# A recurrent layer's state decay: eight ScalarE activations by head in place of one GpSimd product

## The chip, the cores and the metric

The kernel runs on one core of a Trainium2 chip. The core has five engines with instruction streams of their own: TensorE (PE, with its weight loads PEld), VectorE (DVE), ScalarE (ACT), GpSimd (POOL) and SyncE (SP, which here only issues DMAs). Each engine takes its instructions in order; between engines, semaphores hold an instruction until its inputs are there. The metric is the device time of one execution in microseconds (us), as the median of several runs.

## The reference: what is computed

Three layers follow one another: a recurrent layer with a decaying state (batch 4, 8 heads, 768 steps, head size 48), a mixture of eight experts with a skip test, and a dense layer that multiplies by a clipped gate. The change is in the first:

```python
state = np.zeros((B, H, D, D))
for t in range(S):
    kt, vt, rt = k[:, :, t], v[:, :, t], r[:, :, t]
    cur = np.einsum('bhd,bhe->bhde', u[None] * kt, vt)
    y[:, :, t] = np.einsum('bhd,bhde->bhe', rt, state + cur)
    state = w[None, :, :, None] * state + np.einsum('bhd,bhe->bhde', kt, vt)
```

The decay `w` has one value for each head and each of the 48 rows of the state.

## The kernel before, in words

The recurrence is done in 12 chunks of 64 steps (`C = 64`, `NCH = 12`). Within a chunk the steps are matrix products; from one chunk to the next only the state goes on, multiplied by `w` to the 64th power. The state lies in `SS[c % 2]`, a float32 tile with 112 partitions (48 rows of the state for one pair of batches, 16 unused, 48 rows for the other pair) and 2 x 8 x 48 = 768 elements (two batches side by side, head, column). `T` ("Tpow" in the profile) holds powers of `w` by head, and column 96 of it is the 64th.

For TensorE, VectorE, ScalarE and GpSimd the order of instructions is the order of the program text; the DMAs on SP keep theirs as well. Pass i of the loop over chunks (from line 551) puts in the queues, in this order:

- SP: the store of the rows of chunk i-1 (`store`, L472), the load of values for chunk i+2 (`load_v`, L317).
- `powers(i+2)` (L398): the queries of chunk i+2 are multiplied by powers on GpSimd, the keys on VectorE; both 112 x 1024, in place in `RK`. GpSimd can begin when the load of `RK` (L311) is there.
- `scores(i+1, 0)` on TensorE (L417) and `place(i+1, 0)` on VectorE (L422), which copies them under masks from PSUM tile `at` into `ZZ`. There is one `at`, so the next scores wait for the copies.
- `bonus(i+2)` on ScalarE (L404): eight activations, one for each head, 112 x 128 each, with a scale for each partition. They read what GpSimd made in `powers`.
- `chunk(i)`: `grow` (L431, key-value products into PSUM tiles `sp`), `state` on VectorE (L438): the new state is `sd` + `sp`; then `inner` (L451), which writes the output banks `yp`.
- `settle` on ScalarE (L458), `logits(i-2)` (matmuls L492, copies on ScalarE L494), the loads of the next `KN` and `RK` on SP.
- `scores(i+1, 1)`, `place(i+1, 1)`; `keys(i+2)` on GpSimd (L409).
- `decay(i+1)` (L444): `sd` is the new state times its decay. It is done for i+1 = 1 to 10, ten times. The next reader of `sd` is `state(i+1)`, one pass later.
- `turn(i-1)` on TensorE (L478), then `split(i-1)`: `xh` on ScalarE (L484) and `xl` on VectorE (L485).
- `outer(i)` on TensorE (L464), the state's share of the output, and `evac(i)` on ScalarE (L469), which empties `yp` into `xs`; the next `inner` has to wait for it.

In passes 7 to 10 the routing of the first tokens is worked out besides, mainly on VectorE (L79 to L195), and in passes 9 to 11 ScalarE begins to split weights of the first expert (L706, L708, in the function `unit`). When the loop ends, the experts follow (to about 313 us of the profile), and then the dense layer.

Of the kernel before, what the change touches and what calls it, by code (L numbers as in the profile page):

```python
# [15 lines left out]
AF = mybir.ActivationFunctionType  # L16
ALU = mybir.AluOpType
# [3 lines left out]
B, H, S, D = 4, 8, 768, 48  # L21
# [184 lines left out]
class Kernel:  # L206
# [70 lines left out]
    def attention(self):  # L277


        nc, tc = self.nc, self.tc  # L280
        with ExitStack() as ctx:
# [14 lines left out]
            SS = [flat(t) for t in S_]  # L296
            ZZ = [cst.tile([128, 2, H, C], F32, name=f"ZZ{i}") for i in range(2)]
            sd = cst.tile([112, 2, H, D], F32, name="sd")
# [48 lines left out]
            T = cst.tile([112, H, 128], F32, name="Tpow")  # L347
# [18 lines left out]
                                        inv[:, :, i:i + 1].to_broadcast([112, H, n]), op=ALU.mult)  # L366
                n, i = 2 * n, i + 1
            PRb = T[:, :, 0:64].unsqueeze(1).to_broadcast([112, 2, H, C])
            dec = T[:, :, 96:97].unsqueeze(1).to_broadcast([112, 2, H, D])
            uw = cst.tile([112, H], F32, name="uw")  # L370

            mask = self.mask
# [68 lines left out]

            def decay(c):

                nc.gpsimd.tensor_tensor(sd, SS[c % 2], dec, op=ALU.mult)  # L444

            def inner(c, yp):

# [103 lines left out]
            for i in range(NCH):  # L551
# [48 lines left out]
                if not last and i + 1 < NCH - 1:  # L600
                    decay(i + 1)
# [712 lines left out]
```

## Time and profile before

| what | value |
|---|---|
| time, median of 3 runs (lowest to highest) | 680.26 us (676.86 to 681.88) |
| the profiled execution: its own time | 687.5 us |
| its span, from the first to the last instruction | 685.6 us |
| instructions | 15680 |
| busy share of the span: PE, DVE, ACT, POOL | 92%, 57%, 47%, 17% |

A busy share is an average over stages with different limits. "Idle before, releaser" is the time for which an engine stood still ahead of an instruction, and what ended it. "Issue" is time in which an engine waited for nothing that the profile shows. The granted clock of TensorE is given as a share of its full 2.4 GHz; the lower of its two levels is 1.2 GHz, and a mean between 0.5 and 1 is a mix of the two.

### The profile page before, as it was taken

To read this page: it belongs to the slowest core of one execution; us is meant where nothing else is said; L and a number is where in the kernel's file an instruction comes from. 1 tells how busy PE (TensorE), PEld (TensorE's weight loads), DVE (VectorE), ACT (ScalarE), POOL (GpSimd) and SP (SyncE) were. 2 spreads that over 40 slices of the span, in tenths; PEclk is the share of its full clock that TensorE was granted. 3 is DMA by queue.
4 is the path that set the end of the run, shared out by engine and by line. 5 is a ranking of instruction groups with operands and counts; after the bars stand their busy time and mean duration, and the time that the engine had idled before them with its cause. 6 is when DMAs were issued, how large, how long until landed. Compare 5 with 4: busy or idle time off the path is not lost.

```text
span 685.6 us, 15680 instructions
## 1 busy us (share of the span) xinstructions
PE 632.0 (92%) x6728; PEld 406.2 (59%) x6728; DVE 392.6 (57%) x643; ACT 319.7 (47%) x603; POOL 119.9 (17%) x83
## 2 busy tenths in 40 slices
PE   8687777687998999999999999999999999999996
PEld 4576766675776777755555555555555555555553
DVE  7565447959488998479974343334334343434332
ACT  2354434584477656354563344335433533443332
POOL 4675644433721113100000000000000000000000
PEclk9688567889999999999999999999999999999999
DMA  8987885173868777155512010201010010002002
GB/s 249 274 225 215 211 217 159 49 230 123 313 233 297 269 258 253 52 169 206 187 45 46 1 35 12 46 1 47 7 41 1 1 44 3 1 1 47 1 0 47
DMA packets 25229, 79.13 MB, mean 115 GB/s; under 512 B 3906, under 2 KB 13252, under 8 KB 23364
## 3 DMA queue, kind: packets, MB, share of 16 engines
q1 hardware_dynamic: 22964, 70.22, 33.5%
q0 software_dynamic: 2192, 7.87, 3.3%
q8 instruction: 54, 0.88, 0.5%
q14 instruction: 19, 0.16, 0.1%
HBM read 65.49 MB, written 12.58 MB: 114 GB/s over the span
## 4 chain that ended last, share of the span: by engine, by line
PE 65%; DVE 13%; DMA 11%; issue 6%; ACT 3%; SPq 1%; POOL 0%; POOLq 0%; DVEq 0%; ACTq 0%
PE a L1110 26%; PE y L1128 13%; PE s L1128 13%; DMA raw<-in_w 5%; PE at L417 4%; DVE wl L711 4%; DMA X<-xg,icol 2%; PE g L478 2%; PE y L464 2%; PE y L451 2%; PE s L431 1%; DMA xg<-X,icol 1%; DVE ZZ L422 1%; ACT wh L706 1%; DVE hl L758 1%
## 5 line engine op out<-in xcount | busy, mean ns | idle before, releaser
L1110 PE MATMUL a<-x,wih 128*128 128x512 f16 x480 | 142.8, 379 | 0.0
L1115 DVE SCALAR_TENSOR_TENSOR g<-r,a 128x512 f32<-128x512 f32 x96 | 65.9, 686 | 133.9 <-ACT r L1113 133.9
L1113 ACT ACTIVATE r<-a,half_c 128x512 f32<-128x512 f32 x96 | 65.7, 685 | 126.1 <-PE a L1110 126.0
L1128 PEld LDWEIGHTS <-gh 128*128 128x128 f16 x768 | 75.1, 98 | 54.5
L1119 ACT ACTIVATE gh<-g 128x512 f16<-128x512 f32 x96 | 60.6, 631 | 86.8 <-DVE g L1115 86.8
L1120 DVE SCALAR_TENSOR_TENSOR gl<-g,gh 128x512 f16<-128x512 f32 x96 | 66.3, 691 | 57.9 <-ACT gh L1119 57.9
L1110 PE MATMUL a<-x,wil 128*128 128x512 f16 x240 | 91.0, 379 | 0.0
L1110 PEld LDWEIGHTS <-wih 128*128 128x128 f16 x576 | 55.5, 98 | 55.7 <-issue 0.2
L753 PE MATMUL a<-mx,wh 128*128 128x128 f16 (+1 forms) x576 | 68.0, 241 | 3.7 <-DVE hl L758 2.8
L1128 PE MATMUL y<-woh,gl 128*128 128x384 f16 x192 | 62.6, 326 | 0.3 <-DVE gl L1120 0.3
L1128 PE MATMUL y<-woh,gh 128*128 128x384 f16 x192 | 62.6, 326 | 0.0
L1128 PE MATMUL y<-wol,gh 128*128 128x384 f16 x192 | 62.6, 326 | 0.0
L1128 PE MATMUL s<-woh,gh 128*128 128x384 f16 x192 | 62.6, 326 | 0.0
L1128 PE MATMUL s<-woh,gl 128*128 128x384 f16 x192 | 62.6, 326 | 0.0
L1128 PE MATMUL s<-wol,gh 128*128 128x384 f16 x192 | 62.6, 326 | 0.0
L753 PE MATMUL a<-mx,wl 128*128 128x128 f16 (+1 forms) x288 | 60.4, 241 | 0.0
L711 DVE SCALAR_TENSOR_TENSOR wl<-raw,wh 128x768 f16<-128x768 f32 x57 | 52.8, 966 | 9.2 <-ACT wh L706 9.1
L422 DVE COPY_PREDICATED ZZ<-mask,at 128x512 f32<-128x512 uint8 x48 | 35.2, 734 | 38.6 <-PE at L417 37.7
L706 ACT ACTIVATE wh<-raw 128x768 f16<-128x768 f32 x64 | 50.9, 838 | 11.8 <-DMA raw<-in_w 11.6
L1128 PEld LDWEIGHTS <-gl 128*128 128x128 f16 x384 | 37.6, 98 | 30.4 <-DVE gl L1120 0.9
L753 PEld LDWEIGHTS <-wh 128*128 128x128 f16 x576 | 49.6, 99 | 9.9 <-issue 3.4
L417 PE MATMUL at<-RK 48*64 48x128 f32 x768 | 39.4, 353 | 12.7 <-DVE ZZ L422 8.2
(199 smaller groups left out, 969.4 us busy)
## 6 DMA issues: line engine op xcount, KB each, us to landing
raw<-in_w SPq DMA_DIRECT2D x13, 1536.0 KB, 6.8
RK<-in_rkT SPq DMA_DIRECT2D x32, 192.0 KB, 5.9
draw<-in_win SPq DMA_DIRECT2D x8, 768.0 KB, 5.0
draw<-in_wout SPq DMA_DIRECT2D x8, 768.0 KB, 4.3
KN<-in_kn SPq DMA_DIRECT2D x12, 384.0 KB, 6.1
VV<-in_vn SPq DMA_DIRECT2D x12, 384.0 KB, 4.8
X<-xs SPq DMA_DIRECT2D x12, 384.0 KB, 4.2
out<-o SPq DMA_DIRECT2D x48, 96.0 KB, 2.2
```

The lines of the kernel that those rows point to most:

```text
L417: nc.tensor.matmul(at[tok(b), TG[b], j], x[dim(b), 1, DG[b], h], x[dim(b), 0:3:2, DG[b], h], start=True, stop=True)
L422: nc.vector.copy_predicated(ZZ[c % 2][:, :, 4 * hh:4 * hh + 4], mask[:, m].unsqueeze(1).unsqueeze(1).to_broadcast([128, 2, 4, C]), at[:, : ...
L451: nc.tensor.matmul(yp[b // 2][out(b), h], z[tok(b), TG[b], h], v[tok(b), cols(TG[b], h)], start=h == 0, stop=c == 0 and h == H - 1, skip_g ...
L706: nc.scalar.activation(hi, src, AF.Copy, scale=SW)
L711: nc.vector.scalar_tensor_tensor(lo, src, SW, hi, op0=ALU.mult, op1=ALU.subtract)
L753: nc.tensor.matmul(hp[:, j], a[:, kc, fs], b[:, kc], start=(k == 0), stop=(k == 8))
L1110: nc.tensor.matmul(hp, a[:, g, kc, fs], b[:, kc], start=(k == 0), stop=(k == 8))
L1113: nc.scalar.activation(r, hp, AF.Relu, scale=1.0 / (6.0 * SX * SW2), bias=self.half_c)
L1115: nc.vector.scalar_tensor_tensor(g, r, 1.0, hp, op0=ALU.min, op1=ALU.mult)
L1119: nc.scalar.activation(gh, g, AF.Copy, scale=SGG / (SX * SW2))
L1120: nc.vector.scalar_tensor_tensor(gl, g, SGG / (SX * SW2), gh, op0=ALU.mult, op1=ALU.subtract)
L1128: nc.tensor.matmul(yps[t], a[:, ts_], b[:, f], start=(f == 0 and i == 0), stop=(f == NF2 - 1 and i == 2))
```

## The change

The product on GpSimd goes; in its place in the text ScalarE gets eight activations, each for one head: it reads the two 48-element runs of that head from the state, multiplies by the head's decay as a scale for each partition, and writes the same places of `sd`. Shape 112 x 96, float32 in and out. Nothing else is changed.

```diff
@@ attention()
             PRb = T[:, :, 0:64].unsqueeze(1).to_broadcast([112, 2, H, C])
-            dec = T[:, :, 96:97].unsqueeze(1).to_broadcast([112, 2, H, D])
             uw = cst.tile([112, H], F32, name="uw")
@@ decay(c)
             def decay(c):
 
-                nc.gpsimd.tensor_tensor(sd, SS[c % 2], dec, op=ALU.mult)
+                for h in range(H):
+                    nc.scalar.activation(sd[:, :, h], SS[c % 2][:, :, h], AF.Copy, scale=T[:, h, 96:97])
```

## Rows read from the trace of the kernel before

**Rows 1.** Three windows: PE, PEld, DVE, ACT, POOL busy us (count), PE clock, DMA share, GB/s.

```profile
12.00:142.00 130.00, 95.34 (x2967) 85.54 (x2967) 83.68 (x141) 58.59 (x184) 75.63 (x38) 0.72 0.68 193
142.00:313.00 171.00, 159.42 (x1629) 119.07 (x1629) 132.83 (x223) 101.29 (x166) 41.97 (x34) 0.97 0.66 227
313.00:686.00 373.00, 367.09 (x2067) 197.00 (x2066) 168.19 (x251) 155.04 (x245) 0.00 (x0) 1.00 0.12 33
```

**Rows 2.** Instructions on tile sd: durations in ns (min/median/max); who waited, us, times.

```profile
L444 POOL TENSOR_TENSOR sd<-SS,Tpow x10: 1500/1502/1509, 24.5 to 124.4; 112x768 f32<-112x768 f32 x10
...
  POOL sd L444: 17.5, 6
```

**Rows 3.** Groups by line, GpSimd, 12 to 142 us: busy us, mean ns, idle before.

```profile
L398 POOL TENSOR_TENSOR RK<-RK,Tpow 112x1024 f32<-112x1024 f32 x11 | 29.0, 2637 | 30.5 <-DMA RK<-in_rkT 24.4 <-PE y L464 4.2 <-ACT xs L469 1.8
```

**Rows 4.** Groups by line, ScalarE, 12 to 142 us.

```profile
L404 ACT ACTIVATE RK<-RK,uw 112x128 f32<-112x128 f32 x88 | 26.9, 390 | 25.7 <-POOL RK L398 25.7
...
L484 ACT ACTIVATE xh<-g 128x384 f16<-128x384 f32 x20 | 9.4, 489 | 24.2 <-PE g L478 23.2
L706 ACT ACTIVATE wh<-raw 128x768 f16<-128x768 f32 x6 | 4.9, 834 | 0.0
```

**Rows 5.** Timeline of ScalarE, 12 to 165 us: start, length, instruction [idle before <-releaser].

```profile
22.53 2.45 ACT L404 ACTIVATE RK<-RK,uw 112x128 f32<-112x128 f32 x8 [2.60 <-POOL RK L398]
...
36.25 0.87 ACT L484 ACTIVATE xh<-g 128x384 f16<-128x384 f32 x2
37.66 0.86 ACT L469 COPY xs<-y 128x384 f32<-128x384 f32 x2 [0.54 <-PE y L464]
...
45.24 0.49 ACT L484 ACTIVATE xh<-g 128x384 f16<-128x384 f32 x1 [0.92 <-PE g L478]
...
47.80 0.86 ACT L469 COPY xs<-y 128x384 f32<-128x384 f32 x2 [1.42 <-PE y L464]
...
55.16 0.17 ACT L458 COPY seen<-y 128x8 f32<-128x8 f32 x1 [2.33 <-PE y L451]
...
58.27 0.49 ACT L484 ACTIVATE xh<-g 128x384 f16<-128x384 f32 x1 [2.56 <-PE g L478]
...
66.94 0.87 ACT L484 ACTIVATE xh<-g 128x384 f16<-128x384 f32 x2 [1.33 <-PE g L478]
...
89.78 0.87 ACT L484 ACTIVATE xh<-g 128x384 f16<-128x384 f32 x2 [1.51 <-PE g L478]
91.19 0.86 ACT L469 COPY xs<-y 128x384 f32<-128x384 f32 x2 [0.54 <-PE y L464]
...
125.61 0.87 ACT L484 ACTIVATE xh<-g 128x384 f16<-128x384 f32 x2 [1.27 <-PE g L478]
127.02 0.86 ACT L469 COPY xs<-y 128x384 f32<-128x384 f32 x2 [0.54 <-PE y L464]
```

**Rows 6.** Timeline of SP's DMA issues, around the first store.

```profile
28.54 0.40 SPq L472 DMA_DIRECT2D X<-xs  x1
```

**Rows 7.** Timeline of VectorE, pass 2: the first masked copies.

```profile
39.28 1.52 DVE L422 COPY_PREDICATED ZZ<-mask,at 128x512 f32<-128x512 uint8 x2
```

**Rows 8.** Timeline of TensorE, pass 2: inner products, then the second scores.

```profile
39.25 1.12 PE L451 MATMUL y<-VV,ZZ 64*64 64x64 f32 x63
...
42.67 1.09 PE L417 MATMUL at<-RK 48*64 48x128 f32 x27 [1.39 <-issue]
```

**Rows 9.** Chain that ended last, 119 to 142 us: start, length, what.

```profile
126.67 0.91 DVE xl L485 x2
...
134.64 1.99 PE at L417 x32
```

**Rows 10.** The same chain after the loop, in the experts' stage.

```profile
172.67 10.02 DMA raw<-in_w
```

**Rows 11.** Instructions that read Tpow: durations in ns (min/median/max).

```profile
L398 DVE TENSOR_TENSOR RK<-RK,Tpow x13: 1208/1218/2205, 8.0 to 120.7; 112x1024 f32<-112x1024 f32 x13
L398 POOL TENSOR_TENSOR RK<-RK,Tpow x11: 2340/2372/3337, 14.1 to 115.2; 112x1024 f32<-112x1024 f32 x11
```

## The prediction

> **What bounds the kernel now.** I read the windows by stage first, to see where the change can matter at all. From 313 us on TensorE is busy 367.1 of 373 us; in the experts before that it is busy 159.4 of 171; in the stretch from 12 to 142 us, where the chunks of the recurrence run, it is busy only 95.3 of 130, at a mean granted clock of 0.72, that is a mix of its levels 2.4 and 1.2 GHz [rows 1]. All ten decays lie in that stretch. No engine is full there: DVE has 83.7 us, ACT 58.6, POOL 75.6 of 130 [rows 1]. So each pass is a ring of waits between engines, and a change counts only where it lengthens or shortens the wait that ends last in its pass.
>
> Next I read the tile that the change writes. The ten products take 1.50 us each, evenly from 1500 to 1509 ns, and the view's list of waiting instructions has one entry: GpSimd's own decay waited 17.5 us for the new state. VectorE's `state`, the only reader of `sd`, is not in the list [rows 2]. The result is there long before it is wanted.
>
> Then the two engines between which work moves. GpSimd stood still 30.5 us ahead of `powers`, 24.4 of it for the DMA that brings `RK` [rows 3]. ScalarE stood still 25.7 us ahead of `bonus`, for GpSimd, and 24.2 us ahead of the 20 `xh` of `split`, nearly all of it for TensorE's transposes [rows 4]. The new instructions stand in ScalarE's order just ahead of those `xh`. Last I read the timeline of ScalarE, to see how large that hole is in each pass [rows 5], and the chain, to see in which pass VectorE's work behind `xh` sets the pace [rows 9].
>
> **The change part by part.**
>
> *Taken from GpSimd*: ten times 1.50 us, 15.0 us [rows 2]. Its next instruction is `powers` of the next pass, which waits for a DMA [rows 3], so GpSimd only waits longer there. Nobody waited for `sd` but GpSimd itself. Gain on the path: 0. If `RK` came earlier, at most 1.5 us of a pass could be won, but then `bonus` behind it would also have to be what ScalarE waits for last.
>
> *Added to ScalarE: the price of one burst.* The trace has no 112 x 96 activation, but a near relative: `bonus`, also eight in a row with a scale for each partition, 112 x 128, takes 2.45 us for eight [rows 5] at 390 ns each [rows 4], so one follows the other every (2.45 - 0.39) / 7 = 0.294 us. The cost of an element I bound from the 128 x 768 activation: (834 - 390) / (768 - 128) = 0.69 ns [rows 4]. With 32 elements fewer a burst is 7 x (0.294 - 0.022) + 0.368 = 2.27 us. Bounds: 2.45 us if elements cost nothing, 2.45 x 96 / 128 = 1.84 us if they cost everything. I take 2.3, as the fixed part is what `bonus` shows to dominate. Ten bursts are 23 us, and ScalarE goes from 58.6 to about 82 of 130 us, 63%: more, but not the bound. The Trainium skill speaks against the change here: the page "ScalarE: Activation LUTs" (section "What ACT_TABLE_LOAD costs") charges every activation a fixed 186 ns, 93 ns more for each pointer operand, 0.833 ns for an element, with 93 ns of overlap between neighbours. By its figures a burst would be an estimated 7 x 0.266 + 0.359 = 2.2 us, ten 22 us, which the 390 ns of [rows 4] bear out to within 1% (386 by the page).
>
> *Where each burst lies.* It begins when ScalarE has done `settle` and `logits` and the new state is there, and holds back `xh` of the same pass, then `evac`; behind `xh` on VectorE are `xl`, `powers` and `place` of the next pass, and behind `place` the next scores on TensorE; behind `evac` are the next store, the next `bonus` and the next `inner`. Pass by pass, with 2.3 us:
>
> - Pass 0: behind `bonus`, which ends at 24.98 [rows 5], to 27.3. It delays `evac(0)` by 2.3 to about 28.1. The store that reads its result is issued only at 28.54 [rows 6]: covered, cost 0. Without that cover it would be 2.3.
> - Pass 1: no idle time ahead of `xh` at 36.25 and 0.54 ahead of `evac` at 37.66 [rows 5]. So `xh` comes at 38.55 and `evac(1)` at 39.4, 1.8 late, done at 40.3. `inner(2)`, at 39.25 [rows 8], must wait for it: 1.0 late. VectorE: `xl` ends near 40.1, `powers` (1.22 [rows 11]) at 41.3, so `place` starts 2.0 late instead of at 39.28 [rows 7] and ends at 42.8. The second scores wait for it; before, 27 of 32 ran only from 42.67 because of 1.39 us of issue [rows 8]. If that hole stays at its time, 0.1 is lost; if it comes after the wait, 1.7. I take 0.6, nearer the low end, since the hole is not tied to `place`.
> - Pass 2: a hole of 0.92 ahead of `xh`; the burst runs from 44.32 to 46.6, `xh` ends at 47.5, and `evac` was only to start at 47.80 [rows 5]. Cost 0. In pass 3 `settle` waits 2.33 for TensorE, so the `bonus` ahead of it may also come that much later.
> - Passes 3, 5 and 7: holes of 2.56, one of which stands in [rows 5]: the burst fits. Pass 8: its wait for TensorE is longer. Cost 0.
> - Pass 4: a hole of 1.33, `xh` 1.0 late; pass 6: 1.51, `xh` 0.8 late, `evac` 0.8 - 0.54 = 0.3 late [rows 5]. For both I take 0.2 together, the `evac` alone, mostly covered by the time that `inner` leaves.
> - Pass 9: a hole of 1.27 [rows 5], so `xh` 1.0 and `evac` 0.5 late. Here VectorE is the chain: `xl`, then the routing up to `place`, then the scores at 134.64 [rows 9]. `xl` started at 126.67 behind other VectorE work [rows 9]; the first `xh` would now end at 124.34 + 2.27 + 0.49 = 127.1. Cost 0.5, on the path.
>
> Sum: -0 + 0 + 0.6 + 0.2 + 0.5 = +1.3 us. After the loop the chain goes over weight loads whose buffers come free with splits of passes 9 and 10, such as the 10.02 us load at 172.67 [rows 10]; I let the whole 1.3 through. The profiled execution took 687.5 us (685.6 of span), so it would take 688.8; it stands 7.2 above the median of the runs, and on the median's scale the forecast is 680.3 + 1.3 = 681.6 us.
>
> **The rivals.**
>
> *The delays are handed on (slower).* Mechanism: a late `xh` makes `xl`, `powers` and `place` late, `at` stays full, and TensorE's scores wait in each pass. For it: pass 1 and pass 9 show just that path. Against it: issue holes and waits for TensorE leave a pass slack again. Price if all lateness is passed on: 2.3 (pass 0) + 2.3 + 1.4 + 1.0 + 0.8 + 1.0 (passes 1, 2, 4, 6, 9) = 8.8 us, 689.1. It decides, that is exceeds 1%, once 6.8 of the 8.8 are passed on; TensorE at its upper level more of the time would help it, since the holes ahead of `xh` are then shorter.
>
> *VectorE is freed (faster).* GpSimd and VectorE do hinder each other: VectorE's `powers` takes 1208 ns alone and up to 2205, GpSimd's 2340 up to 3337 [rows 11]. If each decay held a VectorE instruction for such a 1.0 us, taking ten away would give 10 us, 670.3. Against it: the decays never took more than 1509 ns [rows 2], so none of them met such a neighbour in this execution. The Trainium skill ("SBUF — State Buffer", section "Terms") says that the port pair shared by VectorE and GpSimd is held for a whole instruction, while ScalarE has its own; by that rule a gain of up to ten times 1.5 us would be possible. The trace agrees for `powers` and shows no such case for the decay.
>
> *Nothing happens.* GpSimd had idle time and ScalarE has it; every burst is swallowed, pass 9 included, because VectorE catches up in the waits of passes 10 and 11: 680.3 us.
>
> **How the numbers follow.** The forecast (0 to 3 us lost, so 680 to 683) gets 0.60, nothing happens 0.14, delays handed on 0.19, VectorE freed 0.07. About 1%, 6.8 us, is what a measurement of this kernel can tell from no change. Of the 0.19, some 0.06 falls short of it, so slower has 0.13, the same 0.60 + 0.14 + 0.06 = 0.80, faster 0.07. The range goes up to the full price of the slower case, 689, and down to 676.5, just under the lowest of the runs (676.9), as runs of one kernel scatter by 5 us; outside are the freed VectorE and a slower case worse than its price, together under 0.2.
>
> **What would show it.** Right: eight activations of about 0.37 us each for one pass, a burst of 2.2 to 2.4 us; the idle time ahead of `xh` down from 24.2 us by some 18; GpSimd idle for `RK` up; `state` still not waiting for `sd`; the window of the chunks longer by 1 to 2 us. Wrong: `place` and the scores waiting in most passes and a window longer by more than 5 us (delays handed on); VectorE's `powers` or copies shorter than before (freed); or a burst well off 2.3 us, for instance if the two runs of 48 elements cost extra. The time is also wrong if TensorE's granted clock over the chunks moves away from 0.72, or the issue holes fall elsewhere: neither follows from the change, and either is worth a few us.

## The result and the profile after

The changed kernel takes 684.46 us (median of 20 runs, 679.53 to 688.49), the kernel before 681.39 us (20 runs, 676.86 to 687.12). The ratio is 1.0052, 95% interval 1.0031 to 1.0072: 3.5 us slower (2.1 to 4.9), within the 1% called "the same", on the side that was forecast, but more than the 1.3 us of the sum. The profiled execution has a span of 682.6 us, less than that of before (685.6); single executions scatter by more than the effect, so the traces are read here for what waits for what, and the times for how much.

The same three windows as in [rows 1], of the kernel after:

```profile
12.00:142.00 130.00, 91.51 (x3036) 81.62 (x3037) 87.80 (x143) 79.35 (x267) 59.68 (x28) 0.77 0.70 196
142.00:313.00 171.00, 158.57 (x1579) 117.48 (x1578) 134.14 (x225) 101.81 (x165) 43.64 (x34) 0.99 0.65 227
313.00:683.00 370.00, 364.33 (x2053) 195.63 (x2051) 164.58 (x246) 153.34 (x243) 0.00 (x0) 1.00 0.12 33
```

ScalarE goes from 58.6 to 79.4 of 130 us, GpSimd from 75.6 to 59.7; still no engine is full. The activations, on tile sd as in [rows 2]:

```profile
L444 ACT ACTIVATE sd<-SS,Tpow x80: 358/360/381, 26.8 to 123.3; 112x96 f32<-112x96 f32 x80
```

The groups of ScalarE and GpSimd by line, 12 to 145 us, answering [rows 3] and [rows 4] (line 404 has become 403, 398 has become 397):

```profile
L403 ACT ACTIVATE RK<-RK,uw 112x128 f32<-112x128 f32 x88 | 26.9, 390 | 25.2 <-POOL RK L397 25.2
L444 ACT ACTIVATE sd<-SS,Tpow 112x96 f32<-112x96 f32 x80 | 22.3, 363 | 7.4 <-DVE SS L437 7.4
L484 ACT ACTIVATE xh<-g 128x384 f16<-128x384 f32 x22 | 10.0, 479 | 6.4 <-PE g L478 5.7
...
L397 POOL TENSOR_TENSOR RK<-RK,Tpow 112x1024 f32<-112x1024 f32 x11 | 26.2, 2380 | 48.3 <-DMA RK<-in_rkT 39.2 <-PE y L464 6.2 <-ACT sd L444 2.8
```

Three things are to be seen. The 15 us taken from GpSimd have become waiting: 48.3 us ahead of `powers` in place of 30.5. The idle time ahead of `xh` has shrunk from 24.2 to 6.4 us; the bursts lie in that hole. And the burst has a wait of its own: 7.4 us in four passes for the new state, on VectorE (L437, `state`). Before, `xh` did not depend on the state; now it stands behind it in ScalarE's order.

Who waited for whom, 12 to 145 us, after (us in total, times, longest):

```profile
PE at L416 <- DVE ZZ L421: 10.6, 6, 4.5
...
DVE xl L485 <- ACT xh L484: 4.6, 4, 2.0
```

TensorE's scores waited 10.6 us in six passes for the masked copies (before 8.2 in four), and VectorE 4.6 us in four passes for `xh` (before 0.5 in one). These four are passes 1, 2, 6 and 9. ScalarE's timeline in passes 1 and 9, after, to hold against [rows 5]:

```profile
37.68 0.21 ACT L458 COPY seen<-y 128x8 f32<-128x8 f32 x2
37.78 2.24 ACT L444 ACTIVATE sd<-SS,Tpow 112x96 f32<-112x96 f32 x8
39.92 0.85 ACT L484 ACTIVATE xh<-g 128x384 f16<-128x384 f32 x2
40.66 0.85 ACT L469 COPY xs<-y 128x384 f32<-128x384 f32 x2
...
119.87 0.25 ACT L136 COPY rkA<-g 128x104 f32<-128x104 f32 x1 [0.36 <-PE g L132]
121.39 2.24 ACT L444 ACTIVATE sd<-SS,Tpow 112x96 f32<-112x96 f32 x8 [1.27 <-DVE SS L437]
123.53 0.84 ACT L484 ACTIVATE xh<-g 128x384 f16<-128x384 f32 x2
124.28 0.84 ACT L469 COPY xs<-y 128x384 f32<-128x384 f32 x2
```

In both passes `seen` or the state is followed by burst, `xh` and `evac` with no hole between them. In pass 9 the chain that ended last now runs over the burst (after, 12 to 165 us, to hold against [rows 9]):

```profile
120.40 0.91 DVE SS L437 x2
...
121.39 0.70 ACT sd L444 x3
...
123.63 0.38 ACT xh L484
124.03 1.02 DVE xl L485 x2
...
128.13 2.52 DVE vA L175
...
132.11 1.99 PE at L416 x32
```

### The profile page after: what moved, and what is told of

Same layout as the page of the kernel before. It is cut to its first block, busy times and chain, and to the rows that moved or that the text cites. A ratio compares the mean times of both kernels' runs of the same rounds, so it can differ in the third digit from the quotient of the medians.

```text
span 682.6 us, 15737 instructions
## 1 busy us (share of the span) xinstructions
PE 624.4 (91%) x6728; PEld 399.2 (58%) x6728; DVE 394.7 (58%) x643; ACT 339.3 (50%) x683; POOL 105.6 (15%) x73
## 4 chain that ended last, share of the span: by engine, by line
PE 65%; DMA 14%; DVE 10%; issue 5%; ACT 3%; POOL 1%; SPq 0%; POOLq 0%; ACTq 0%
PE a L1110 27%; PE y L1128 14%; PE s L1128 14%; DMA X<-xg,icol 6%; DMA raw<-in_w 4%; PE at L416 3%; DVE wl L711 2%; DMA KN<-in_kn 2%; PE y L464 2%; PE y L451 2%; PE g L478 1%; DMA xg<-X,icol 1%; PE g L730 1%; DVE ZZ L421 1%; ACT wh L706 1%
## 5 line engine op out<-in xcount | busy, mean ns | idle before, releaser
L753 PE MATMUL a<-mx,wh 128*128 128x128 f16 (+1 forms) x576 | 65.9, 237 | 3.2 <-DVE hl L758 2.3
L753 PE MATMUL a<-mx,wl 128*128 128x128 f16 (+1 forms) x288 | 59.0, 237 | 0.0
L416 PE MATMUL at<-RK 48*64 48x128 f32 x768 | 35.2, 328 | 15.1 <-DVE ZZ L421 10.6
```

Source lines behind the costliest of these rows:

```text
L416: nc.tensor.matmul(at[tok(b), TG[b], j], x[dim(b), 1, DG[b], h], x[dim(b), 0:3:2, DG[b], h], start=True, stop=True)
L753: nc.tensor.matmul(hp[:, j], a[:, kc, fs], b[:, kc], start=(k == 0), stop=(k == 8))
```

## The experiments

The theory, "place": the loss comes from where the burst stands, ahead of `xh` and `evac`. Rivals: "amount" (22 us more work on ScalarE cost the same wherever they stand) and "freed" (GpSimd's missing products themselves give or cost time). Ratios are to the kernel before, run beside the others of its group, with 95% intervals; 0.001 is about 0.7 us. The groups differ (the kernel before took 689.65, 682.28 and 689.54 us in the three below), so only ratios are compared.

**The burst behind `evac`.**

```diff
-                if not last and i + 1 < NCH - 1:
-                    decay(i + 1)
 ...
                 evac(xs, yp)
+                if not last and i + 1 < NCH - 1:
+                    decay(i + 1)
```

> The eight activations stay on ScalarE, but stand behind evac instead of ahead of split, that is in the hole in which ScalarE waits for the bonus of the next pass (25 us idle in the chunks' stretch). Theory 'place' (the loss comes from xh and evac being held back): ratio to before 1.000, between 0.998 and 1.002. Rival 'amount' (22 us more work on ScalarE cost the same wherever they stand): 1.005 as in the changed kernel. Rival 'freed' (GpSimd's missing products themselves give or cost time): the ratio of the kernel without any decay, not 1.000.

Measured: 1.0074 (1.0044 to 1.0105), no better than the changed kernel. In its simple form "place" falls: the time ahead of `bonus` is not free either. The trace shows two spots where work that other engines wait for now stands behind the burst. In pass 8 it is the `Exp` of the routing (L100), for which VectorE waits 3.95 us (before 1.9); in pass 9 it is the split of the first weights, and there the chain runs over the burst. The two rows of pass 8, from the timelines of ScalarE and VectorE, and the chain in pass 9:

```profile
118.12 0.27 ACT L100 ACTIVATE exA<-exA 128x96 f32<-128x96 f32 x1
118.42 0.25 DVE L106 TENSOR_REDUCE seA<-exA 128x12 f32<-128x96 f32 x1 [3.95 <-ACT exA L100]
...
128.37 0.48 ACT xs L469
128.85 2.12 ACT sd L444 x8
130.97 0.74 ACT wh L706
131.74 0.84 ACT raw L708
132.58 0.74 ACT wh L706
133.35 0.84 ACT raw L708
134.19 0.12 ACT seen L458 x2
```

ScalarE works without a hole from `evac` of pass 9 to `settle` of pass 10, and the burst is 2.1 us of that.

**No decay at all.**

```diff
-                if not last and i + 1 < NCH - 1:
-                    decay(i + 1)
+            nc.gpsimd.memset(sd, 0.0)        # once, at the start
```

> The decay is left out: sd is set to zero once and the state is not carried on with its decay, so no engine does this work. Theory 'place' and rival 'amount': GpSimd only waits longer for RK, ratio to before 1.000 (0.998 to 1.002). Rival 'freed': below 0.997 if GpSimd's products held something up (by their 15 us at most 0.978), above 1.003 if their absence costs time.

Measured: 0.9995 (0.9966 to 1.0024). "Freed" falls: the missing 15 us on GpSimd neither give nor cost anything that can be seen. It also says how much there is to win with the decay: leaving it out gains at most 0.3%, so a place for it that cost nothing could hardly gain more.

**Both engines do it.** The product stays on GpSimd, and ScalarE does the burst besides, into another tile.

```diff
                 nc.gpsimd.tensor_tensor(sd, SS[c % 2], dec, op=ALU.mult)
+                for h in range(H):
+                    nc.scalar.activation(sd2[:, :, h], SS[c % 2][:, :, h], AF.Copy, scale=T[:, h, 96:97])
```

> GpSimd's product as before, and besides it the eight activations of each pass into a second tile that nobody reads, at the same place in ScalarE's order. Theory 'place' and rival 'amount': the loss of the changed kernel, ratio 1.005 (1.003 to 1.007), since only what is added counts. Rival 'freed': another ratio, 1.008 and more if the changed kernel won something back on GpSimd, below 1.002 if GpSimd's missing work caused the loss.

Measured: 1.0038 (1.0009 to 1.0067), the loss of the changed kernel within the interval. The loss is what ScalarE got, not what GpSimd lost.

**The burst twice.**

```diff
-                for h in range(H):
-                    nc.scalar.activation(sd[:, :, h], ...)
+                for t in (sd2, sd):
+                    for h in range(H):
+                        nc.scalar.activation(t[:, :, h], ...)
```

> The changed kernel with the burst done twice in each pass, the first time into a second tile that nobody reads: 16 activations, 4.4 us in place of 2.2, ahead of xh. Theory 'place': the holes ahead of xh are used up by the first burst (24.2 us idle before, 6.4 after), so the second 21 us are handed on in larger part than the first: 10 to 20 us more than the changed kernel, ratio to before 1.02 to 1.035. If only passes 1 and 9 pay, as the prediction had it: 2 x 2.1 = 4 us more, 1.011. If the loss has nothing to do with ScalarE's order: 1.005.

Measured: 1.0129 (1.0074 to 1.0183), 8.9 us, that is some 5 us for the second 21 us of work. That is less than "handed on in larger part" asked for, and fits the expectation that a few passes pay in full. VectorE waits for `xh` in nearly every pass now, five times as long as in the changed kernel (who waited for whom, 12 to 150 us):

```profile
DVE xl L487 <- ACT xh L486: 23.5, 9, 3.9
...
PE at L417 <- DVE ZZ L422: 11.8, 7, 3.9
```

But TensorE's scores wait for the copies hardly longer, 11.8 us against 10.6: between `xl` and `place` most passes have the room that the prediction counted on.

**Which passes pay.** Three kernels have the burst on ScalarE in some passes alone, enlarged so that it can be measured; GpSimd does the rest.

```diff
                 nc.gpsimd.tensor_tensor(sd, SS[c % 2], dec, op=ALU.mult)
+  # in the passes named, in its place: the burst n times, all but the last into sd2
+                for t in [sd2] * (n - 1) + [sd]:
+                    for h in range(H):
+                        nc.scalar.activation(t[:, :, h], SS[c % 2][:, :, h], AF.Copy, scale=T[:, h, 96:97])
```

> Only in passes 0 to 2 the decay is on ScalarE, there with the burst done twice (4.4 us, the first into a tile that nobody reads); from pass 3 on GpSimd does it as before. Theory 'first passes pay': most of the 9 us of the kernel with ten double bursts comes from here, ratio 1.006 and more. Theory of the prediction (pass 0 covered, pass 1 in part, pass 2 covered): the second 2.2 us come through in pass 1 alone, 0.6 + 2.2 = 2.8 us, 1.004. Rival 'middle' or 'pass 9': 1.001 or less.

Measured: 1.0038 (1.0004 to 1.0073), 2.6 us; the expectation from the prediction was 2.8.

> Only in passes 3 to 8 the decay is on ScalarE, with the burst done twice; GpSimd does the others. Theory 'middle pays': each of these passes gives a little, together more than half of the 9 us, 1.006 and more. Theory of the prediction (holes of 2.5 us ahead of xh, then slack before place): 6 x (4.4 - 2.5) = 11 us of lateness, of which the issue holes swallow most; 0 to 3 us, 1.002.

Measured: 1.0014 (0.9983 to 1.0045), 1.0 us for six passes with 4.4 us of burst each. The middle passes swallow nearly all of it, as the prediction had it.

> Only in pass 9 the decay is on ScalarE, with the burst done three times (6.6 us); GpSimd does the others. Theory 'pass 9 is the path': the first burst costs 0.5 to 1.0 us, each further one its full 2.1, together 4.7 to 5.3 us, ratio 1.007 to 1.008. If VectorE catches up later (nothing happens): 1.002 or less.

Measured: 1.0101 (1.0053 to 1.0150), 6.9 us for three bursts in one pass. Pass 9 passes on what it gets: the interval is 3.6 to 10.2 us and holds both the 4.7 to 5.3 that were expected and the 6.6 of three whole bursts. With the run before, "amount" falls: by the intervals twelve bursts in the middle passes cost at most 3.1 us, three in pass 9 at least 3.6. Its chain, with 24 activations in one piece between the routing's copy and `xh`:

```profile
124.06 0.24 ACT rkA L136
124.30 3.76 ACT sd L448 x15
...
128.19 2.48 ACT sd L448 x9
130.67 0.38 ACT xh L490
...
131.08 1.02 DVE xl L491 x2
132.10 0.08 DVE cnts L143
```

**The burst behind `evac` in passes 0 to 7, GpSimd in 8 and 9.**

```diff
                 evac(xs, yp)
+                if i < 8:
+                    decay(i + 1)      # on ScalarE; in passes 8 and 9 on GpSimd, at the old place
```

> The burst stands behind evac in passes 0 to 7, where its result and ScalarE's next work are not on the chain of the first experiment; in passes 8 and 9, where that chain went through the burst (ahead of the routing's Exp and of the weight split, 2.1 us each), GpSimd does the decay. Theory 'place': the loss of 1.007 goes away, ratio 0.998 to 1.002. Rival 'amount' (8 of 10 bursts are still on ScalarE): 1.004 to 1.006.

Measured: 1.0020 (0.9990 to 1.0050). By its middle it is the "place" expectation, but the interval holds that of "amount" as well. It is no faster than the kernel before.

**The last four, in one group.** The changed kernel again; the changed kernel with pass 9 left to GpSimd; pass 9 alone on ScalarE; and all bursts between `split` and `evac`, so that `xh` is not held back.

```diff
+                if c < 10:        # all but pass 9; the third kernel has c == 10 here
+                    for h in range(H): nc.scalar.activation(sd[:, :, h], ...)
+                else:
                     nc.gpsimd.tensor_tensor(sd, SS[c % 2], dec, op=ALU.mult)
```

> The changed kernel once more, beside the others on one chip: ratio 1.003 to 1.007, as measured at first.

Measured: 1.0037 (1.0006 to 1.0068).

> The changed kernel, but in pass 9 GpSimd does the decay. Theory 'pass 9 and the first passes pay': pass 9 alone gives back 0.5 to 1.0 us of the 3.5, so this is 2.5 to 3 us above before, ratio 1.003 to 1.0045. If pass 9 holds nearly all of the loss: 1.001 or less.

Measured: 0.9990 (0.9956 to 1.0024): without pass 9 nothing of the loss is seen, more than the theory gave to pass 9. It is one more sign against "amount", by which nine of the ten bursts cost nine tenths of the loss, 1.0033 to 1.0047 by the two measurements of the changed kernel.

> Only pass 9 has its decay on ScalarE, once. Theory: 0.5 to 1.0 us, ratio 1.0007 to 1.0015; in the trace the burst lies on the chain between state and xh, and the first xl comes 0.5 to 1.0 us later after the masked copies than in the kernel before. If pass 9 holds nearly all of the loss: 1.004 to 1.005.

Measured: 1.0003 (0.9972 to 1.0033). Alone, pass 9 does not show the loss that its absence takes away. The two do not add up to 1.0037 by their middles, only within their intervals. In the trace `xl` waits 0.84 us for `xh` in that pass, as expected.

```diff
                     split(i - 1)
+                if not last and i + 1 < NCH - 1:
+                    decay(i + 1)      # behind split, ahead of evac
```

> All ten bursts on ScalarE, but behind split and ahead of evac, so that xh and xl are not held back and only evac is, by 2.2 us less its idle time (0.5 to 2.5). Theory 'place': pass 9 no longer pays, since its chain goes over xl; evac's delay is taken up by the 2 us before the next inner in most passes; pass 1 still pays a part. 0 to 2 us, ratio 1.000 to 1.003. Rival 'amount': 1.005 as in the changed kernel.

Measured: 1.0021 (0.9982 to 1.0060), within what was expected of "place", but not told apart from "amount".

**What the profiles say of pass 9.** Times of single passes are too small for the intervals above, but the profiles, one for each kernel, can be laid side by side. From the timelines of VectorE, GpSimd, TensorE and ScalarE, in us: from the end of the masked copies ahead of `state` in pass 9 to the first instruction behind `xl` (L143); the length of `vA` (L175), the longest step of the routing; the start of GpSimd's first weight subtraction (L709 of the kernel before, `wl`) less the start of `vA`; the next scores of TensorE (32 matmuls, L417 of before); `outer` of pass 9 on TensorE (64 matmuls, L464 of before), for which `evac` waits; and from `evac` of pass 8 to `evac` of pass 10.

| kernel | burst ahead of `xh` in pass 9 | copies to L143 | `outer` | `vA` | `wl` less `vA` | scores | `evac` 8 to 10 |
|---|---|---|---|---|---|---|---|
| changed | once | 4.58 | 1.16 | 2.60 | -1.24 | 1.99 | 23.86 |
| changed, again | once | 4.60 | 1.16 | 2.60 | -1.26 | 1.98 | 23.93 |
| both engines | once | 4.57 | 1.16 | 2.60 | -1.24 | 1.98 | 23.86 |
| pass 9 alone | once | 4.51 | 1.16 | 2.60 | -1.25 | 1.99 | 23.82 |
| all twice | twice | 6.69 | 1.99 | 2.60 | -1.26 | 1.99 | 25.98 |
| pass 9 thrice | thrice | 8.84 | 1.16 | 2.62 | -1.24 | 1.99 | 28.16 |
| before | none | 4.15 | 1.16 | 2.60 | -1.00 | 1.99 | 23.45 |
| behind `evac` in 0 to 7 | none | 3.56 | 1.16 | 2.61 | -1.01 | 1.98 | 22.86 |
| behind `evac` | none | 4.55 | 1.99 | 1.15 | 2.51 | 1.64 | 26.42 |
| no decay | none | 4.48 | 1.99 | 1.15 | 0.30 | 1.10 | 21.35 |
| passes 0 to 2 twice | none | 3.55 | 1.99 | 1.14 | 0.25 | 1.10 | 19.94 |
| passes 3 to 8 twice | none | 3.55 | 1.99 | 1.16 | 0.04 | 1.10 | 19.87 |
| all but pass 9 | none | 3.66 | 1.99 | 1.17 | 0.39 | 1.10 | 20.18 |
| behind `split` | none | 3.55 | 1.99 | 1.14 | 0.62 | 1.10 | 20.26 |

The first column of numbers shows the price of the place: 4.5 to 4.6 with one burst, 6.69 with two, 8.84 with three, so each further burst costs its whole 2.1 us. What the first costs depends on TensorE. Without a burst the column is 3.55 to 3.66 in the five kernels in which VectorE waited 0.33 us for the second scores of the pass, ahead of its second copies; it is 4.15 in the kernel before, where it waited 0.92, and 4.48 and 4.55 where it waited 1.27 and 1.21. So the first burst costs 0.9 to 1.0 us where VectorE is early, and 0.4 against the profile of the kernel before.

The other columns show something else. In all six kernels with the burst there, `vA` takes 2.60 to 2.62 us and the scores 1.98 to 1.99; in six of the eight without, 1.14 to 1.17 and mostly 1.10. VectorE's timeline of the changed kernel (run again) and of the one with pass 9 on GpSimd:

```profile
125.90 2.60 DVE L175 TENSOR_TENSOR vA<-oh2A,vals 128x960 f16<-128x960 f16 x1
```

```profile
127.62 1.17 DVE L175 TENSOR_TENSOR vA<-oh2A,vals 128x960 f16<-128x960 f16 x1
```

And TensorE, the same two kernels, 108 to 145 us, `outer` of pass 9 first:

```profile
120.80 1.16 PE L464 MATMUL y<-SS,RK 48*64 48x64 f32 x64
...
128.56 0.98 PE L182 MATMUL g<-vA,ohl 128*128 128x80 f16 x12 [2.42 <-DVE vA L175]
129.97 1.98 PE L416 MATMUL at<-RK 48*64 48x128 f32 x32 [0.43 <-DVE ZZ L421]
131.88 1.54 PE L478 MATMUL g<-c,xs 128*128 128x128 f32 x6
133.35 2.03 PE L464 MATMUL y<-SS,RK 48*64 48x64 f32 x64
```

```profile
123.44 1.99 PE L468 MATMUL y<-SS,RK 48*64 48x64 f32 x64
...
129.88 0.59 PE L182 MATMUL g<-vA,ohl 128*128 128x80 f16 x12 [0.73 <-ACT lg L498]
130.40 1.10 PE L417 MATMUL at<-RK 48*64 48x128 f32 x32
131.44 0.87 PE L482 MATMUL g<-c,xs 128*128 128x128 f32 x6
132.24 1.16 PE L468 MATMUL y<-SS,RK 48*64 48x64 f32 x64
```

With the burst, `evac` follows `xh` at once, and the weight split behind it starts early against VectorE, which came late by the burst. So GpSimd's subtraction `wl`, which waits for that split, begins 1.26 us ahead of `vA` and not 0.39 behind it, and `vA` takes 1.4 us longer. GpSimd in the two kernels:

```profile
124.64 6.97 POOL L709 TENSOR_TENSOR wl<-raw,wh 128x768 f16<-128x768 f32 x3 [13.03 <-ACT raw L708]
```

```profile
128.01 5.51 POOL L713 TENSOR_TENSOR wl<-raw,wh 128x768 f16<-128x768 f32 x3 [4.59 <-ACT raw L712]
```

TensorE, which waits for `vA`, stands idle 2.4 us, and then runs the scores, the transposes and `outer` in 1.98, 1.54 and 2.03 us in place of 1.10, 0.87 and 1.16, 2.4 us more. The granted clock is the third number from the end of a window's row; over these three steps it is 0.55 with the burst in pass 9 and 1.00 without, that is nearly the lower level of 1.2 GHz against the upper one:

```profile
128.50:135.40 6.90, 6.38 (x114) 5.27 (x114) 6.30 (x22) 2.40 (x4) 5.32 (x4) 0.55 0.13 35
```

```profile
129.80:133.40 3.60, 3.52 (x114) 2.98 (x113) 3.53 (x14) 2.99 (x6) 3.60 (x3) 1.00 0.01 2
```

Together these are 1.0 + 1.4 + 2.4 = 4.8 us, of which 3.6 to 4 arrive in the last column.

But the two profiles differ in one thing more, ahead of all this. Without the burst it is `outer` that decides when `evac` starts, and so when the split and `wl` do. `outer` of pass 9 in the kernel before (`evac` waits 0.54 us for it, [rows 5]), and `evac` in the kernel with pass 9 on GpSimd:

```profile
125.83 1.16 PE L464 MATMUL y<-SS,RK 48*64 48x64 f32 x64
```

```profile
125.46 0.86 ACT L473 COPY xs<-y 128x384 f32<-128x384 f32 x2 [1.42 <-PE y L468]
```

In the two kernels without the burst in which `outer` took 1.16 us (granted clock 1.00), `evac` started 0.45 us after `xl`, and `vA` met `wl`. In the six in which it took 1.99 us (0.50, the lower level), `evac` started 1.5 to 2.1 us after `xl`, and `vA` was alone (in "behind `split`" the burst holds `evac` back besides). With the burst, `evac` started 0.24 us after `xl` in all six, with `outer` at 1.16 us in five of them and at 1.99 in one ("all twice"). The burst of pass 9 does not set that level: `outer` does not wait for it, and the changed kernel and the one with pass 9 on GpSimd are the same program up to there.

So like has to be held against like. Where `outer` took 1.16 us, the last column is 23.8 to 23.9 with one burst and 22.9 and 23.5 without: the burst costs 0.4 to 1.1 us, and the meeting of `vA` and `wl` is there either way. Where it took 1.99, there is no profile with one burst; from the two bursts of "all twice" one would take an estimated 26.0 - 2.1 = 23.9 us, 3.6 to 4 more than the 19.9 to 20.3 of four of the kernels without. What the burst would add there is that `vA` meets `wl` at the lower level too, which is shown for two bursts only. How often each level comes in pass 9 is not known, and no kernel here was made to keep `wl` apart from `vA` with the burst in place.

## Why the prediction was right, and where its size was not

- *Taken from GpSimd, gain 0*: right. No decay at all gives 0.9995, and GpSimd waits 48.3 us for `RK` and others in place of 30.5. VectorE's `state` still does not wait for `sd`.
- *The burst's price, 2.27 us, bounds 1.84 to 2.45*: right; 2.22 to 2.24 us in the timeline, 360 ns for one. The Trainium skill's "ScalarE: Activation LUTs" (section "What ACT_TABLE_LOAD costs") led to 359 ns and 2.2 us; the trace agrees.
- *The holes ahead of `xh`, down by some 18 us*: right, 24.2 to 6.4.
- *Pass 0 covered, passes 3 to 8 nearly covered*: for passes 3 to 8 borne out, 1.0 us (-1.2 to 3.1) with the burst even doubled. Pass 0 was not measured by itself; in the profile after, `evac(0)` ends at 29.81 and the store is issued at 29.83, so there the store waited for it, and what that costs is not known.
- *Pass 1, 0.6 us, within 0 to 1.7*: its steps came as worked out. From the start of `bonus` in that pass to `xh` it is 39.92 - 35.33 = 4.59 us, against 38.55 - 33.63 = 4.92 in the working; from the same start to the end of the second scores it is 45.89 - 35.33 = 10.56 us, against 43.76 - 33.63 = 10.13 before, 0.4 longer. That it comes so near to 0.6 is partly luck: the issue hole of 1.39 us is gone, and VectorE's `powers` takes 1.96 us in place of 1.22. Passes 0 to 2 together cost 2.6 us with the burst doubled, where 2.8 was expected; what one burst costs there the runs don't resolve.
- *Pass 9, 0.5 us, on the path*: the right place, and as far as the profiles tell the term that is too small. On the execution from which it was worked out it holds: 4.58 against 4.15 us, 0.4. Where VectorE waits less for the second scores, the same burst costs 1.0. And the sum stopped at the scores that follow. It did not ask what the later VectorE and the weight split would run beside: with the burst `vA` meets GpSimd's `wl` in each of the six profiles, which is 1.4 us, and the longer wait of TensorE is followed by its lower level. The execution on which the sum was made had that meeting already (`outer` 1.16, `vA` 2.60, `wl` 1.00 earlier), as had one of seven other profiles without the burst. A sum against that execution could not see it as a loss.
- *The window of the chunks longer by 1 to 2 us*: not to be read from single executions. The last `evac` starts at 146.97 us after and at 148.32 before, and the mean granted clock from 12 to 142 us is 0.77 and not 0.72; a change of the clock was named there as worth a few microseconds.
- *Nothing of the sum is given back after the loop*: borne out by the profiles. From `evac` of the last pass to the end of the span it is 535.6 and 537.3 us for the first two kernels, and by groups 542.2 to 545.2, 534.8 to 536.0 and 541.9 to 544.1, whatever the loop did.
- *The rival "VectorE is freed"* ended as it was weighed: no gain at the decay. But its mechanism came in from the other side. The Trainium skill ("SBUF — State Buffer", section "Terms") says that VectorE and GpSimd share a port pair which one holds for a whole instruction while the other is blocked; `vA` grew from 1.15 to 2.60 us beside `wl`, an addition of 1.45 us that is shorter than the 1.64 us of one `wl` alone, so the trace agrees.
- *The delays are handed on (8.8 us)*: not as a whole. Most passes took them up, and only double bursts reached 8.9 us. *Nothing happens* did not come either: the interval of 2.1 to 4.9 us leaves zero out. It reaches into the forecast of 0 to 3 us, but not down to the sum of 1.3.

What stays open is how the 3.5 us divide. Pass 9 left out of the change gives 0.9990, so by that it holds nearly all; pass 9 alone gives 1.0003, so by that almost nothing. Both intervals are some 0.7% wide. The profiles show two prices for its burst, 0.4 to 1.1 us and an estimated 3.6 to 4, by TensorE's level in `outer`, and each profile is one execution. Nor do whole loops show the difference: the last `evac` starts at 143.69 us in the changed kernel run again and at 143.78 in the one without pass 9. So where the forecast was short, pass 9 is the likely place, and how it comes to 3.5 us on average is not shown.

No kernel tried beats the one before by more than its interval; the one with no decay at all, the one without pass 9 and the one with pass 9 alone are equal to it.

## What to carry to other kernels

Moving work to an engine with idle time costs nothing only where the idle time lies in the same pass and behind the same inputs: list the holes pass by pass, and add to the moved work the wait for its own operand, which everything behind it on the new engine inherits. A delay of a microsecond on an engine off the bound can change which instructions of VectorE and GpSimd run side by side later, so look behind the delayed one for the next pair like `vA` and `wl` here, two products with both inputs in SBUF. And before a sum is made on a single execution, see whether the pass that carries the largest term is in its usual form there.

## What the runs showed of the hardware that was not expected

- VectorE's `vA` (128 x 960, fp16, two inputs in SBUF) takes 1.14 to 1.17 us alone and 2.60 to 2.62 us when GpSimd's subtraction (128 x 768, fp32 less fp16) has begun 1.0 to 1.3 us before it; nothing between was seen in 14 profiles.
- After 1.5 to 3.7 us of waiting for `vA`, TensorE's 32 score matmuls took 1.98 to 1.99 us in each of eight profiles, close to the lower clock level; where it waited 0.4 to 1.3 us, 1.10 us in each of five; in the fourteenth, behind 2.4 us of waiting for ScalarE, 1.64.
- The 64 matmuls of `outer` in pass 9 took 1.16 us in seven profiles (granted clock 1.00) and 1.99 in the other seven (0.50), on different sides also for two kernels that are the same program up to there.
- The same kernel took 1% longer in some groups of runs (681.4 and 682.3 us against 689.5 and 689.7), and in the profiles that time lies behind the loop of the chunks. Why is not known.
